# Two small sync-queue loads for 16 partitions of one weight piece in a decode kernel

## The chip, the core and the metric

The kernel runs on one core of a Trainium2 chip. Its time is the device time of one execution in microseconds (us); the figure used is the median over several runs. The core has a matrix engine (PE, with its weight loads PEld), a vector engine (DVE), a scalar engine (ACT), a general engine (POOL) and a sync engine (SP). Transfers between HBM and the on-chip memory SBUF (128 partitions) are issued from SP, ACT or POOL, each with a queue of its own, and are carried out by 16 DMA engines which all queues share. In the profile SP's queue is q1 ("hardware_dynamic"), POOL's is q0 ("software_dynamic"), and q8 and q14 ("instruction") carry the program's own instructions.

## What is computed

The input `x` is 4 rows of 576. It is normalised to `xn`, and the result is the sum of `x`, an attention branch and an MLP branch:

```
xn = layernorm(x)
A: q = xn @ wq ; scores over the last 2048 keys of 16 kv heads ; softmax ; p @ v ; @ wo
B: x1 = xn + hs ; h2 = gelu(layernorm(x1) @ w3) @ w4 ; return x1 + h2
out = x + A + B
```

With one token per sequence the shifted part `hs` of branch B is zero, so `w1` and `w2` are not needed. What the kernel must read is therefore `wq` (4.7 MB), keys and values (67 MB), `wo` (4.7 MB), `w3` and `w4` (5.3 MB each): 87 MB for a few rows of arithmetic.

## The kernel before, in words

Almost all data come in one long stream on POOL's queue. `flush_loads` issues it in the order of the list `order`: keys and values of eight pairs of heads ("K", t and "V", t, each one indirect load of 128 rows of 32 KB, line 125) into three buffers, a quarter of `wo` before every second V (line 147), `w3` after the second V (lines 152 and 153), and last the entry ("W", 0): the last quarter of `wo` and all of `w4`. An entry is issued when a K or V buffer comes free; `free_one`, called twice in each turn of the main loop, says so. SP issues only the two loads of `wq` at the start (lines 142 and 143) and the store of the result at the end (line 716).

`w4` has 4608 rows of 576. Seen as 2 x 128 x 18 rows, each partition holds 36 of them, numbered 0 to 35 in the tile. `load_w4` (line 158) brings them in six pieces, cut at `W4_PIECES` (line 156): rows 0-17, 18-24, 25-29, 30-33, 34 and 35 of every partition. A row is 1152 bytes, so the second piece (number 1) is 7 rows, 8064 contiguous bytes for each of 128 partitions.

The tiles of `wq`, `w3` and `w4` share one buffer (pool `wp`, one buffer, tag "w"), which each takes over from the one before. `w3` is read by `mlp_g` (line 529) in turn `t == G_AT`, that is turn 3 of the main loop; the last of its reads is `mlp_g(2)`. The step `mlp_turn(2)` and the gelu `mlp_act` follow some microseconds later in the same turn. From there on the buffer is empty until `w4` comes.

The end of the kernel is written out by hand (lines 643 to 716). After the last head's values are turned and projected, the matmuls with `w4` follow piece by piece, so that each waits for its own piece only:

```
acc_matmuls(mlp_terms(*W4_PIECES[0:2]))
...
acc_matmuls(mlp_terms(*W4_PIECES[1:3]))
half = sum_open()
sum_matmuls(mlp_terms(*W4_PIECES[2:4]), first=True)
sum_fold(half)
sum_matmuls(mlp_terms(W4_PIECES[3], NF))
```

Then DVE and ACT each copy half of the result (lines 713 and 715) and SP stores it.

Of the kernel before, what the change touches and what calls it, by code (L numbers as in the profile page):

```python
# [11 lines left out]
BF16 = mybir.dt.bfloat16  # L12
# [10 lines left out]
def kernel(  # L23
# [14 lines left out]
    nc = tc.nc  # L38
    P = 128
    B, Sq, D = A_x.shape  # L40
# [4 lines left out]
    F = B_w3.shape[1]  # L45
    assert Sq == 1 and Dh == P and rep == 2 and B == 4 and D == 576
    KJ = 4
    NQ = Hq * Dh
    NF = F // P
    NFH = NF // 2  # L50
# [27 lines left out]
    wp = ctx.enter_context(tc.tile_pool(name="w", bufs=1))  # L78
# [12 lines left out]
    w_tiles = {}  # L91
# [62 lines left out]
        w_tiles["w3"] = t  # L154

    W4_PIECES = [0, NFH, NF - 11, NF - 6, NF - 2, NF - 1, NF]

    def load_w4():
        t = wp.tile([P, NF, D], BF16, tag="w", name="w4_sb")
        src = B_w4.rearrange("(e p i) n -> e p i n", e=2, p=P)  # L160
        for lo, hi in zip(W4_PIECES, W4_PIECES[1:]):
            e, at = divmod(lo, NFH)
            nc.gpsimd.dma_start(out=t[:, lo:hi, :], in_=src[e][:, at:at + hi - lo, :])  # L163
        w_tiles["w4"] = t

    order = [("K", 0), ("K", 1)]
    for t in range(NPR):
# [126 lines left out]
    def k_transpose(t, q):  # L294
        src = kv_tiles["K", t][:].bitcast(I32)[:, q * QC:(q + 1) * QC, :].rearrange("p c (ib i) -> p ib c i", i=QD)
        kt = ktp.tile([P, 2, QC, QD], I32, tag="kt")
        nc.vector.transpose(out=kt[:], in_=src)  # L297
        kts[t, q] = kt
# [3 lines left out]
    for kb in range(NQD):  # L302
        nc.gpsimd.tensor_copy(out=sel[:, :, :, kb, :],
                              in_=ident_bf[:].rearrange("p (ib i e) -> p ib e i", ib=2, e=2))
# [23 lines left out]
    for g in range(2):  # L328
        nc.gpsimd.tensor_copy(out=same_j[:, g * 2 * QD:(g + 1) * 2 * QD].rearrange("p (e s j) -> p e s j", e=2, j=NJ),
                              in_=sel_j[:].unsqueeze(2).to_broadcast([P, 2, NSL, NJ]))  # L330
# [41 lines left out]
    for r in range(2):  # L372
        nc.vector.tensor_copy(out=q_bf[:, r],  # L373
                              in_=qT_ps[:, r].rearrange("p u (g x) -> p g u x", g=NQD)[:, :, :, 0:B])
    qs_ps = ps_m.tile([P, Hkv, 4, rep, B], F32, tag="m", name="qs_ps")
    for ie in range(4):
        ib, e = divmod(ie, 2)
        nc.tensor.matmul(out=qs_ps[:, :, ie], lhsT=sel[:, ib, e].rearrange("p k i -> p (k i)"),
                         rhs=q_bf.rearrange("p r g u b -> p (r g u b)"), start=True, stop=True)
    for kb in range(NQD):  # L380
        rows = slice(kb * QD, (kb + 1) * QD)
        dst = qz[rows, ZP:].rearrange("p (t i m) -> p t i m", i=4, m=P)[:, :, :, kb * QD:kb * QD + NJ]
        src = qs_ps[rows].rearrange("p (t e) i r b -> p e t i (r b)", e=2)[:, kb // 2]
# [13 lines left out]
    def k_mask(t, u):  # L397
        S_ps[t, u] = ps_s.tile([P, NW], F32, tag="S", name="S")
        nc.tensor.matmul(out=S_ps[t, u][:].rearrange("p (c k) -> p c k", k=QD), lhsT=ohT[:],  # L399
                         rhs=negbig[:].unsqueeze(1).to_broadcast([B, SC, QD]),  # L400
                         start=True, stop=False, skip_group_check=True)

    def k_scores(t, q, sl):
        u, s = q // 2, q % 2 * 2 + sl
        kt = kts[t, q][:].bitcast(BF16)
        if sl:
            kts.pop((t, q))
        for ie in range(4):
            ib, e = divmod(ie, 2)
            z0 = (t * 4 + ie) * P + ZP - s * NJ  # L410
            nc.tensor.matmul(out=S_ps[t, u][:], lhsT=qz[:, z0:z0 + P],  # L411
                             rhs=kt[:, ib, sl * SC:(sl + 1) * SC, e:2 * QD:2].rearrange("p c k -> p (c k)"),
                             start=False, stop=False, skip_group_check=True)

    def sm_max(t, u):
        mx = small.tile([P, 1], F32, tag="mx")
        nc.vector.reduce_max(out=mx[:], in_=S_ps[t, u][:], axis=AX.X)  # L417
        if u == 0:
            st["dm", t] = small.tile([P, NU, NG], BF16, tag="dm", name="dm")
        nc.vector.tensor_scalar(out=st["dm", t][:, u, :], in0=sel_g[:], scalar1=mx[:, 0:1], scalar2=None, op0=ALU.mult)  # L420
# [7 lines left out]
    def sm_neg(t):  # L428
        nm = small.tile([2 * NJ, 1], BF16, tag="nm")
        nc.vector.reduce_max(out=nm[:], in_=st.pop(("mg", t))[:], axis=AX.X, negate=True)  # L430
        st["nm", t] = nm
# [46 lines left out]
    def o_scale(t):  # L478
        O_sb[t] = bigp.tile([P, NSL, Dh], F32, tag="big", name="O_sb")
        nc.scalar.activation(out=O_sb[t][:], in_=O_ps.pop(t)[:], func=ACT.Copy, scale=st.pop(("rd", t))[:, 0:1])  # L480
# [48 lines left out]
    def mlp_g(r):  # L529
        w3 = w_tiles["w3"]  # L530
        chunks = G_CHUNKS[r * NQD:(r + 1) * NQD]
        n = chunks[0][2]
        g_ps = (ps_o if r < 2 else ps_m).tile([P, P, n], F32, tag="O" if r < 2 else "m", name="g_ps")
        for j in range(KJ + 1):
            for g, (e, i0, _) in enumerate(chunks):
                base, k = (j * F + e * (F // 2), j) if j < KJ else (KJ * F, KJ + e)
                cols = w3[:, base:base + F // 2].rearrange("p (q i) -> p q i", q=P)
                nc.tensor.matmul(out=g_ps[g * QD:(g + 1) * QD], lhsT=ln2T[:, k, :], rhs=cols[:, :, i0:i0 + n],  # L538
                                 start=(j == 0), stop=False, skip_group_check=True)
        m = len(chunks) * QD  # L540
        g_sb[r] = bigp.tile([P, P, n], F32, tag="g", name="g_sb", bufs=1)
        nc.scalar.activation(out=g_sb[r][0:m], in_=g_ps[0:m], func=ACT.Copy)

    def mlp_turn(r):
        chunks = G_CHUNKS[r * NQD:(r + 1) * NQD]
        n, m = chunks[0][2], len(chunks)
        gT_all = ps_m.tile([P, n * m, QD], F32, tag="m", name="gT_ps")
        gT_ps = gT_all[:].rearrange("p (u g) x -> p u g x", u=n)
        gs = g_sb.pop(r)
        for u in range(n):  # L550
            nc.tensor.transpose(out=gT_ps[:, u].rearrange("p g x -> p (g x)"), in_=gs[0:m * QD, :, u],
                                identity=ident_f[0:m * QD, 0:m * QD])
        if r < 2:
            dst = xs[:, r * NFH:r * NFH + 16, :].rearrange("p (g u) b -> p u g b", u=n)
        else:
            dst = xs[:].rearrange("p (g c) b -> p c g b", c=NFH)[:, 16:18]
        nc.vector.tensor_copy(out=dst, in_=gT_ps[:, :, :, 0:B])

    def mlp_act():
        u = const.tile([P, NF, B], F32, name="g_u")  # L560
        nc.gpsimd.tensor_tensor(out=u[:], in0=xs[:], in1=xs[:], op=ALU.mult)
        nc.gpsimd.tensor_scalar(out=u[:], in0=u[:], scalar1=GELU_A, scalar2=1.0, op0=ALU.mult, op1=ALU.add)
        nc.gpsimd.tensor_tensor(out=u[:], in0=u[:], in1=xs[:], op=ALU.mult)
        nc.scalar.activation(out=u[:], in_=u[:], func=ACT.Tanh, scale=GELU_C)
        nc.gpsimd.tensor_scalar(out=u[:], in0=u[:], scalar1=0.5, scalar2=0.5, op0=ALU.mult, op1=ALU.add)
        nc.gpsimd.tensor_tensor(out=gT[:], in0=u[:], in1=xs[:], op=ALU.mult)
# [8 lines left out]
    for t in range(NPR - 1):  # L575
        a, o = t - 1, t - 2
        if a >= 0:
            sm_max(a, 1)
        if o >= 0:
            o_scale(o)  # L580
        k_transpose(t, 1)
        if t == G_AT:
            mlp_g(0)
        k_mask(t, 0)
        k_scores(t, 0, 0)
        if a >= 0:
            sm_maxT(a)
            sm_neg(a)
        k_scores(t, 0, 1)
        if a >= 0:  # L590
            sm_back(a)
            sm_bias(a)
            sm_exp(a, 0)
            sm_exp(a, 1)
        k_transpose(t, 2)
        if t == G_AT:
            mlp_g(1)
            mlp_turn(0)
        k_scores(t, 1, 0)
        if o >= 0:  # L600
            o_turn(o)
        k_scores(t, 1, 1)
        if a >= 0:
            sm_turn(a, 0)
        if o >= 0:
            o_sum(o)
        k_transpose(t, 3)
        free_one()
        if a >= 0:
            sm_turn(a, 1)  # L610
        if t == G_AT:
            mlp_g(2)
            mlp_turn(1)
        k_mask(t, 1)
        k_scores(t, 2, 0)
        if a >= 0:
            sm_den(a)
            sm_rec(a)
            pv(a, 0, 0, SC // 2)
        k_scores(t, 2, 1)  # L620
        sm_max(t, 0)
        if o >= 0:
            o_spread(2 * o + 1)
        if a >= 0:
            pv(a, 0, SC // 2, SC)
        if o >= 0:
            o_pick(2 * o + 1)
        if t == G_AT:
            mlp_turn(2)
            mlp_act()  # L630
        if t + 1 < NPR:
            k_transpose(t + 1, 0)
        k_scores(t, 3, 0)
        if a >= 0:
            pv(a, 1, 0, SC // 2)
        k_scores(t, 3, 1)
        if a >= 0:
            pv(a, 1, SC // 2, SC)
            free_one()
        if o >= 0:  # L640
            o_proj(2 * o + 1)
# [57 lines left out]
    o_spread(2 * hl + 1)  # L699
    acc_matmuls(mlp_terms(*W4_PIECES[0:2]))  # L700
    o_pick(2 * hl + 1)
    o_proj(2 * hl + 1)
# [6 lines that stand above are left out]
# [38 lines left out]
```

## Time and profile before

| | |
|---|---|
| median of 3 runs | 210.86 us (210.72 to 211.22) |
| the profiled execution, its own time | 211.11 us |
| its span, first to last instruction | 209.3 us |
| granted PE clock, mean | 0.876 |
| PE / DVE / ACT / POOL busy | 144.9 / 124.8 / 29.7 / 31.6 us |
| moved by DMA | 87.32 MB, mean 417 GB/s |
| POOL's queue (q0) | 82.45 MB, 91.8% of 16 engines |
| SP's queue (q1) | 4.72 MB, 5.4% of 16 engines |

The span is what the views below are counted in: 0 is the first instruction of the program. The profiled execution's time is 1.8 us more than its span, for what lies around the instructions. "DMA share" is how busy the 16 DMA engines were on average in a stretch. A DMA issue has a length on the engine that issues it, and lands later: the time to landing counts from the issue, so it includes the wait behind all that the queue already holds.

Beside the grouped views the trace keeps a record of each DMA packet (queue, bytes, start and duration, but not which of the 16 engines carried it) and of each completion: a transfer spread over 16 engines has 16 completions, one per engine, and counts as landed with the last.

### The profile page before, as it was taken

What the parts mean: (1) busy time and instruction counts of PE and PEld (TensorE: products, weight loads), DVE (VectorE), ACT (ScalarE), POOL (GpSimd) and SP (SyncE); (2) the same over time, 40 slices, a digit from 0 to 9 for tenths busy, and PEclk for the clock granted to TensorE, in tenths of its full rate; (3) what the DMA queues carried; (4) which work ended last, traced back from release to release, by engine and by line L of the source; (5) the groups of instructions that cost most, each with busy time, mean ns of one, the idle gap of its engine ahead of it and who ended that gap; (6) DMA issues with size and microseconds to landing.
All of it is one profiled execution on the core that took longest, in us unless ns stands there. A gap on an engine that the chain in (4) does not pass through costs nothing.

```text
span 209.3 us, 2197 instructions
## 1 busy us (share of the span) xinstructions
PE 144.9 (69%) x894; PEld 58.4 (28%) x894; DVE 124.8 (60%) x177; ACT 29.7 (14%) x61; POOL 31.6 (15%) x63
## 2 busy tenths in 40 slices
PE   0249199649679943059996894687957937996954
PEld 0013033222215310014442431143314311443432
DVE  5410779994189700097928990989089818987110
ACT  6402500110102011003001201020002010203100
POOL 5680001003200110000133011001010161100000
PEclk9999859996957995558999999597999996997899
DMA  7999999999999999999999999999999999999991
GB/s 301 401 463 438 401 463 423 438 401 451 451 396 437 447 416 413 392 441 482 413 404 465 432 407 409 477 432 407 457 438 404 446 445 413 438 451 401 419 403 70
DMA packets 4155, 87.32 MB, mean 417 GB/s; under 512 B 488, under 2 KB 496, under 8 KB 1200
## 3 DMA queue, kind: packets, MB, share of 16 engines
q0 software_dynamic: 3840, 82.45, 91.8%
q1 hardware_dynamic: 296, 4.72, 5.4%
q8 instruction: 7, 0.11, 0.2%
q14 instruction: 4, 0.03, 0.0%
q10 hardware_dynamic: 8, 0.00, 0.0%
HBM read 87.17 MB, written 0.00 MB: 416 GB/s over the span
## 4 chain that ended last, share of the span: by engine, by line
DMA 62%; PE 18%; DVE 14%; POOL 2%; issue 2%; ACT 0%; POOLq 0%; DVEq 0%
DMA kn<-in_A_k_cache_dram,row 46%; DMA w_sb<-in_B_w_dram 16%; PE S L411 11%; DVE kt L297 9%; PE O L475 6%; DVE pt L456 1%; POOL w_sb L163 1%; DVE mx L417 1%; PE sum L252 1%; POOL vn L125 0%; PE oT L486 0%; DVE on L496 0%; POOL rstd L268 0%; POOL wo_sb L147 0%; DVE row L116 0%
## 5 line engine op out<-in xcount | busy, mean ns | idle before, releaser
L411 PE MATMUL S<-kt,qz 128*128 128x512 bf16 x256 | 78.4, 439 | 33.4 <-DVE kt L297 33.4
L297 DVE STREAM_TRANSPOSE kt<-kn 128x2048 int32<-128x2048 int32 x32 | 73.7, 2307 | 46.5 <-DMA kn<-in_A_k_cache_dram,row 44.2
L411 PEld LDWEIGHTS <-qz 128*128 128x128 bf16 x256 | 23.4, 104 | 72.6 <-issue 55.8
L475 PE MATMUL O<-vn,pt 128*64 128x512 bf16 x256 | 36.0, 412 | 5.5 <-DVE kt L297 2.5
L456 DVE STREAM_TRANSPOSE pt<-E 64x512 bf16<-64x512 bf16 x32 | 22.1, 690 | 1.2 <-ACT E L447 0.9
L447 ACT ACTIVATE E<-S,bias 128x512 bf16<-128x512 f32 x16 | 10.9, 683 | 75.6 <-DVE bias L440 75.6
L125 POOL DMA_INDIRECT vn<-in_A_v_cache_dram,row x8 | 7.7, 961 | 91.6 <-DVE kt L297 87.5
L475 PEld LDWEIGHTS <-pt 128*64 128x64 bf16 x256 | 13.5, 116 | 22.5 <-issue 13.8
L480 ACT ACTIVATE O_sb<-O,rd 128x512 f32<-128x512 f32 x8 | 5.5, 687 | 62.5 <-PE O L475 62.5
L125 POOL DMA_INDIRECT kn<-in_A_k_cache_dram,row x8 | 7.9, 989 | 42.4 <-PE O L475 23.2
L417 DVE TENSOR_REDUCE mx<-S 128x1 f32<-128x512 f32 x16 | 10.7, 668 | 0.1
L538 PE MATMUL g_ps<-w_sb,ln2T 128*32 128x512 bf16 (+1 forms) x50 | 5.2, 486 | 2.9 <-DMA w_sb<-in_B_w_dram 2.9
L399 PE MATMUL S<-negbig,ohT 4*128 4x512 bf16 x16 | 6.4, 398 | 0.0
L486 PE MATMUL oT<-ident_w,O_sb 128*128 128x128 f32 x32 | 5.2, 286 | 0.0
L355 PE MATMUL q_ps<-wq_sb,xnT 128*32 128x512 bf16 x40 | 4.5, 631 | 0.9 <-DMA wq_sb<-in_A_wq_dram 0.9
L496 DVE TENSOR_REDUCE on<-oT 128x16 bf16<-128x128 f32 x8 | 2.3, 287 | 4.4 <-PE oT L486 4.2
L486 PEld LDWEIGHTS oT<-ident_w,O_sb 128*128 128x128 f32 x32 | 4.1, 149 | 2.2 <-issue 0.9
L163 POOL DMA_DIRECT2D w_sb<-in_B_w_dram x6 | 3.3, 585 | 8.2 <-DMA vn<-in_A_v_cache_dram,row 8.2
L440 DVE TENSOR_SCALAR bias<-bp 128x1 f32<-128x1 f32 x8 | 1.3, 158 | 5.2 <-PE bp L435 5.2
L713 DVE CAST fin<-sum 4x288 bf16<-4x288 f32 x1 | 0.4, 446 | 6.5 <-PE sum L252 6.5
L420 DVE TENSOR_SCALAR dm<-sel_g,mx 128x8 bf16<-128x8 bf16 x16 | 3.9, 243 | 0.6
L373 DVE COPY first<-qT_ps 128x64 bf16<-128x64 bf16 x2 | 0.3, 186 | 6.6 <-PE qT_ps L370 6.6
(103 smaller groups left out, 83.1 us busy)
## 6 DMA issues: line engine op xcount, KB each, us to landing
wo_sb<-in_A_wo_dram POOLq DMA_DIRECT2D x4, 1152.0 KB, 23.6
w_sb<-in_B_w_dram POOLq DMA_DIRECT2D x1, 4608.0 KB, 29.5
wq_sb<-in_A_wq_dram SPq DMA_DIRECT2D x1, 4096.0 KB, 13.8
w_sb<-in_B_w_dram POOLq DMA_DIRECT2D x1, 2592.0 KB, 29.1
w_sb<-in_B_w_dram POOLq DMA_DIRECT2D x2, 576.0 KB, 31.7
w_sb<-in_B_w_dram POOLq DMA_DIRECT2D x1, 1008.0 KB, 31.0
w_sb<-in_B_w_dram POOLq DMA_DIRECT2D x1, 720.0 KB, 32.2
wq_sb<-in_A_wq_dram SPq DMA_DIRECT2D x1, 512.0 KB, 3.3
```

The lines of the kernel that those rows point to most:

```text
L125: nc.gpsimd.indirect_dma_start(tl[:].rearrange("p c d -> p (c d)"), None, k_rows if kind == "K" else v_rows, bass.IndirectOffsetOnAxis(ap= ...
L163: nc.gpsimd.dma_start(out=t[:, lo:hi, :], in_=src[e][:, at:at + hi - lo, :])
L297: nc.vector.transpose(out=kt[:], in_=src)
L399: nc.tensor.matmul(out=S_ps[t, u][:].rearrange("p (c k) -> p c k", k=QD), lhsT=ohT[:], rhs=negbig[:].unsqueeze(1).to_broadcast([B, SC, QD] ...
L411: nc.tensor.matmul(out=S_ps[t, u][:], lhsT=qz[:, z0:z0 + P], rhs=kt[:, ib, sl * SC:(sl + 1) * SC, e:2 * QD:2].rearrange("p c k -> p (c k)" ...
L417: nc.vector.reduce_max(out=mx[:], in_=S_ps[t, u][:], axis=AX.X)
L447: nc.scalar.activation(out=E[t, u][:].rearrange("p c k -> p (c k)"), in_=S_ps.pop((t, u))[:], func=ACT.Exp, scale=scale, bias=st["bias", t ...
L456: nc.vector.transpose(out=pts[t % 2 * NU + u][rows, :, e * QD:(e + 1) * QD], in_=e_in[rows])
L475: nc.tensor.matmul(out=O_ps[t][rows], lhsT=pts[t % 2 * NU + u][:, c, :], rhs=vn[:, u, :, c, :], start=(u == 0 and c < 2), stop=False, skip ...
L480: nc.scalar.activation(out=O_sb[t][:], in_=O_ps.pop(t)[:], func=ACT.Copy, scale=st.pop(("rd", t))[:, 0:1])
L486: nc.tensor.transpose(out=oT[:, s, :], in_=o[:, s, :], identity=ident_w[:, s * NJ:s * NJ + P])
L538: nc.tensor.matmul(out=g_ps[g * QD:(g + 1) * QD], lhsT=ln2T[:, k, :], rhs=cols[:, :, i0:i0 + n], start=(j == 0), stop=False, skip_group_ch ...
```

## The change

The piece number 1 of `w4` (rows 18 to 24) is loaded in three parts. Partitions 0 to 111 still come in the stream on POOL's queue, at the same place in the order. Partitions 112 to 119 and 120 to 127 come by two loads of 8 partitions each, issued by SP; in the program they stand in turn 3 of the main loop, between `mlp_turn(2)` and `mlp_act()`. The tile of `w4` is therefore taken there, and no longer in `load_w4`; it has the same number of elements as before (4 x 4608 + 2304 = 36 x 576). The other five pieces and all matmuls are as they were.

```
     W4_PIECES = [0, NFH, NF - 11, NF - 6, NF - 2, NF - 1, NF]
+    W4_LOW = 1
+    LOW = 8
+    w4_src = B_w4.rearrange("(e p i) n -> e p i n", e=2, p=P)
+
+    def w4_load(queue, piece, rows):
+        lo, hi = W4_PIECES[piece:piece + 2]
+        e, at = divmod(lo, NFH)
+        queue.dma_start(out=w_tiles["w4"][rows, lo:hi, :], in_=w4_src[e][rows, at:at + hi - lo, :])
+
+    def load_w4_low():
+        w_tiles["w4"] = wp.tile([P, KJ * F + F // 2], BF16, tag="w", name="w4_sb")[:].rearrange("p (i n) -> p i n", n=D)
+        for p0 in range(P - 2 * LOW, P, LOW):
+            w4_load(nc.sync, W4_LOW, slice(p0, p0 + LOW))
 
     def load_w4():
-        t = wp.tile([P, NF, D], BF16, tag="w", name="w4_sb")
-        src = B_w4.rearrange("(e p i) n -> e p i n", e=2, p=P)
-        for lo, hi in zip(W4_PIECES, W4_PIECES[1:]):
-            e, at = divmod(lo, NFH)
-            nc.gpsimd.dma_start(out=t[:, lo:hi, :], in_=src[e][:, at:at + hi - lo, :])
-        w_tiles["w4"] = t
+        for piece in range(len(W4_PIECES) - 1):
+            w4_load(nc.gpsimd, piece, slice(0, P - 2 * LOW if piece == W4_LOW else P))
...
             mlp_turn(2)
+            load_w4_low()
             mlp_act()
```

## The prediction

> **What bounds the kernel now.** I read first the page's fourth part, the chain that ended last. It gives 62% of the span to DMA.
>
> ```profile
> DMA packets 4155, 87.32 MB, mean 417 GB/s; under 512 B 488, under 2 KB 496, under 8 KB 1200
> ...
> q0 software_dynamic: 3840, 82.45, 91.8%
> q1 hardware_dynamic: 296, 4.72, 5.4%
> q8 instruction: 7, 0.11, 0.2%
> q14 instruction: 4, 0.03, 0.0%
> ...
> DMA 62%; PE 18%; DVE 14%; POOL 2%; issue 2%; ACT 0%; POOLq 0%; DVEq 0%
> ```
>
> The reader should see that one queue, POOL's, fills the 16 DMA engines for 91.8% of the span, and that the program's own instructions take 7 and 4 packets of their own. Next the same chain in order of time, from 164.8 us on:
>
> ```profile
> 169.35 0.94 POOL vn L125
> 170.29 0.00 issue
> 170.29 0.58 POOL wo_sb L147
> 170.87 1.56 POOL w_sb L163 x3
> 172.43 33.10 DMA w_sb<-in_B_w_dram
> 205.54 0.04 issue
> 205.58 1.06 PE sum L252 x12
> 206.63 0.43 DVE fin L713
> ```
>
> From 172.43 us to 205.54 us the chain is the landing of `w4`; after its last byte only 1.06 us of matmuls, the 0.43 us copy and the store remain. So the last of 16 completions, at 205.54, sets the end. Third, the busy time by stretches, near the end (columns: stretch, length, five engines' busy time, PE clock, DMA share, GB/s):
>
> ```profile
> 200.00:205.00 5.00, 3.23 (x78) 2.14 (x79) 0.17 (x1) 0.41 (x1) 0.00 (x0) 1.00 0.94 389
> ...
> 204.00:205.00 1.00, 0.81 (x12) 0.54 (x13) 0.00 (x0) 0.00 (x0) 0.00 (x0) 1.00 0.73 284
> 205.00:206.00 1.00, 0.87 (x12) 0.40 (x10) 0.00 (x0) 0.00 (x0) 0.00 (x0) 1.00 0.32 129
> ```
>
> DMA share falls to 0.73 and then 0.32 before the last byte: the engines don't finish together. The completion records of the last row give it exactly: six engines end at 203.82 to 204.12, two at 204.32 and 204.70, eight at 205.21 to 205.54. Their mean is 204.78.
>
> What made eight engines late shows in the packet records. The first late engine appears right after the 16384-byte instruction packet at 31.98 us (0.93 us, and the next stream packet of that engine 0.83 us instead of 0.35), and each of the 7 packets of q8 and some of q14 adds to one engine. An engine once late by 1.3 to 1.4 us is still late at the end, because the queue is never empty (DMA share 0.99, 1.01 and 0.98 over the first 100, the next 70 and the next 35 us). So time lost by an engine anywhere in mid-stream is there at the end.
>
> **The change, part by part.** *Removed:* one partition in eight of piece 1. Its 128 packets of 8064 bytes took 0.305 us each, 8 on each engine. With 112 rows over 16 engines (my estimate, 112/16 = 7) each engine saves one: -0.305 us.
>
> *Added:* two loads of 8 rows. The four-row loads of this trace (x at the start, the result at the end) gave one packet and one completion to each of four engines. By that row an 8-row load gives one packet of 8064 bytes to each of eight engines; whether both loads use the same eight is not seen, and I take it so. Each of these eight carries two foreign packets in mid-stream and is spared one. Price of one: from below 0.305 us, the stream's own packet of that size; the change from `wq`'s queue to the first keys near 13 us shows no longer packets (1.21 to 1.22 us for 32 KB before and after), so a change of queue can be free. From above the four 8192-byte instruction packets, lone packets of another queue between stream packets: 0.488, 0.309, 0.309 and 0.309 us, and the engine's next 32 KB packet took 1.578, 1.427, 1.579 and 1.744 instead of 1.213. That is 0.85, 0.52, 0.68 and 0.84 us, mean 0.72. This is the nearest row in size, place and kind, so I take 0.72. For eight engines: 2 x 0.72 - 0.305 = **+1.14 us** (ends: +0.305 and 2 x 0.85 - 0.305 = +1.40). For the other eight: -0.305 us.
>
> Which of these reaches the end depends on which engines are late. Eight of sixteen are. The end is moved by +1.14 as soon as one of the latest is among the eight that take the new loads; it falls by 0.305 only if the eight are just the other, early ones, whose 204.70 and 204.12 would then be 205.84 and 205.26 at my price, or 205.01 at the lower. I see no engine numbers in the trace; by chance alone such a clean split is rare.
>
> [...] In this trace the four x rows, which go to four neighbouring partitions at once, took 48 to 56 ns for 1152 bytes each, no more than alone by the stream's rate (1152 / 8064 x 305 = 44 ns, and 9 ns for a mere completion packet), so no crowding is seen, on a very small load. [...]
>
> *Moved: SP.* SP does nothing but wait for the result from the start on.
>
> ```profile
> SPq L716 <- DVE fin L713: 205.5, 1, 205.5
> ```
>
> So the two issues (0.35 us, by the store's issue) delay nobody; the store, behind them on SP, is due 100 us later. They must wait until the buffer's `w3` has been read:
>
> ```profile
> 99.72 1.31 PE L538 MATMUL g_ps<-w_sb,ln2T 128*32 128x256 bf16 x10
> ```
>
> These matmuls end at 101.0, so the loads go out there and run at about 101 to 104 us, amid a stream with DMA share 0.97 (100 to 105 us): there is no idle DMA time to hide in. If SP were later, up to 170 us, the price would be the same.
>
> *POOL.* It issues six `w4` loads as before, and its one wait among them (8.2 us for an earlier value load) stays; that wait ends 24 us before the landing it concerns. A wait for SP's loads, if one is added, was met 65 us earlier: nothing.
>
> *PE.* The 14 matmuls of piece 1 now need three landings. They start at 202.44 us, after 0.66 us of waiting for POOL's part, so the early parts cost nothing; without that cover a met semaphore costs a few hundredths of a microsecond. They end at 203.1, and what follows waits for the later pieces in any case.
>
> Sum: +1.14 us. The profiled execution took 211.11, its span 209.3 plus 1.8 around it, 0.25 above the median; the same shift on the median 210.86 gives **212.0 us**. About 0.2% (0.42 us) is what a measurement of this kernel can tell from no change.
>
> **Rivals.** *(a) The 112-row load runs badly.* The stream's 128-row loads always finish a row in step on all engines; for 112 rows the rows must be dealt out anew, and nothing in the trace shows such a load. [...]
>
> *(b) It evens the engines out, and is not slower.* If all late engines are among the eight that are only spared, the latest end 0.305 earlier: 210.56. It decides at a price per foreign packet below about 0.42 us, because 204.70 + 2p - 0.305 must stay under 205.24; at a mean price of 0.72 the early six (204.12) would reach 205.26 and only the 204.70 engine would pass it, to 205.84. No dealing of the same bytes can gain more than 205.54 - 204.78 = 0.76 us, 210.1. For it: exactly eight engines are late. Against: the instruction packets hit engines one after another, and nothing says they keep to one half.
>
> *(c) Nothing to measure.* The price is at the lower end and late engines lie in both halves: +0.305, 211.2.
>
> **How the numbers follow.** Forecast (+0.5 to +1.4): 0.45. Rival (a), +1.5 to +3.3: 0.18. Rival (b), -0.76 to -0.2: 0.22, of which about 0.12 beyond 0.42 us (that needs more than the worked 0.305, so I count part of it only). Rival (c), within 0.42: 0.15. Slower by over 0.2%: 0.43 of the forecast and all of (a), 0.61; same 0.27; faster 0.12. The range leaves out the best of (b) and the worst of (a): 210.4 to 213.5. The forecast's own range is 211.3 to 212.3.
>
> **What would show it.** In the part on DMA issues, piece 1 at 882 KB (112 x 8064 bytes) and two issues of 63 KB on SPq, landing within a few microseconds of 101; q1 with 32 more packets. The packets after the two loads show whether the next 32 KB packet takes 1.2 or 1.4 to 1.7 us: that is the price. In the last row's completions, the spread of 1.72 us grows to about 2.9 if late engines were loaded, and shrinks below 1.5 under (b). Packets of 8064 bytes near 200 us longer than 0.305 would show (a). The prediction is wrong if foreign packets on SP's queue are cheap, or if the eight engines are just the early ones.

## The result: 217.21 us, and the profile after

The changed kernel took 217.21 us (median of 6 runs, 216.32 to 217.79) beside 210.85 us for the kernel before (6 runs, 210.72 to 211.22): a ratio of 1.0295, 95% interval 1.0278 to 1.0313, so +6.36 us (5.9 to 6.6). The forecast was 212.0 with a range of 210.4 to 213.5: the right sign, and far too little.

The profiled execution took 216.77 us, its span 215.0 plus 1.8 around it; that is 5.66 us more than the profiled execution before. The page's lines on the DMA queues and on the chain that ended last:

```profile
DMA packets 4171, 87.32 MB, mean 406 GB/s; under 512 B 504, under 2 KB 512, under 8 KB 1216
...
q0 software_dynamic: 3824, 82.32, 91.5%
q1 hardware_dynamic: 328, 4.85, 5.5%
q8 instruction: 7, 0.11, 0.2%
q14 instruction: 4, 0.03, 0.0%
...
DMA 63%; PE 23%; DVE 9%; POOL 2%; issue 1%; ACT 0%; POOLq 0%; DVEq 0%
```

The same 87.32 MB move; only the mean rate falls, from 417 to 406 GB/s. q1 has gained 32 packets: 16 of data and 16 completions. The same chain in order of time, its end:

```profile
172.13 0.00 issue
172.14 0.58 POOL wo_sb L147
172.72 1.63 POOL w_sb L164 x3
174.34 36.85 DMA w_sb<-in_B_w_dram
211.20 0.04 issue
211.24 1.07 PE sum L261 x12
212.31 0.43 DVE fin L723
```

The chain is built as before: a landing of `w4`, then 1.07 us of matmuls and the 0.43 us copy. The landing that the chain names is that of rows 30 to 33; rows 34 and 35, for which the last of these twelve matmuls wait, land 0.36 and 0.72 us behind it (205.90 and 206.26 before, 211.58 and 211.93 now), and the copy starts 0.36 us after the last one in both kernels. But the landing in the chain ends at 211.20 and not at 205.54, and those 5.66 us are the whole difference of the two profiled executions. So the question is only why the transfers took longer. What SP waited for, and what the new loads and the shortened one moved, from the page's part on DMA issues:

```profile
SPq L726 <- DVE fin L723: 111.2, 1, 111.2
SPq L164 <- DMA w_sb<-in_B_w_dram: 77.1, 1, 77.1
SPq L164 <- PE g_ps L547: 21.9, 1, 21.9
```

```profile
w_sb<-in_B_w_dram POOLq DMA_DIRECT2D x1, 882.0 KB, 35.1
```

SP waited for `w3`'s landing and its readers, then issued both loads at 100.82 us, and then waited for the result: nothing was behind them. They landed at 108.00 and 111.72 us. The stream's part is 882 KB, 112 rows. The work by stretches (stretch, length, five engines' busy time, PE clock, DMA share, GB/s), first the kernel before and then the changed one, around the two SP loads and around the 112-row load:

```profile
103.00:110.00 7.00, 7.00 (x53) 2.99 (x53) 2.74 (x9) 0.32 (x1) 2.38 (x6) 1.00 0.93 400
197.00:204.00 7.00, 4.29 (x98) 2.81 (x96) 1.43 (x4) 0.90 (x2) 0.00 (x0) 1.00 0.99 414
```

```profile
103.00:110.00 7.00, 7.00 (x52) 2.90 (x50) 2.49 (x9) 0.32 (x1) 2.13 (x6) 1.00 1.00 316
197.00:204.00 7.00, 4.20 (x46) 2.22 (x43) 1.43 (x4) 0.69 (x1) 0.00 (x0) 0.93 0.99 309
```

Read the last two columns together. The DMA share is 1.00 and 0.99, so the engines hardly idle; the rate drops from 400 to 316 and from 414 to 309 GB/s. The packets became longer. The packet records say which (their times are counted from the span's start, as in the views):

- At 104.39 to 105.16 and again at 108.00 to 108.75 eight packets of 8064 bytes of q1 appear, most of them at 0.305 us, the stream's own price. But the 32 KB packet of all 16 engines beside the first load took 2.0 to 2.2 us (one 1.76) instead of 1.21, and beside the second 2.15 to 2.5 (two 1.65 and 2.01). All time of the stream's packets above their usual duration, summed from 103 to 111 us and divided by 16, is 1.80 us per engine.
- The 112 stream packets of 8064 bytes took 0.541 us on average (0.305 to 0.907) instead of 0.305; the pieces beside them suffer too: 5760 bytes 0.348 instead of 0.220, 20,736 bytes up to 1.90 instead of 0.771. It lasts on all engines from the first one that enters the 112-row load (about 199.5) to the last that leaves it (about 207.3). From 195 to 211 us that is 3.30 us per engine.

The last row's completions went from 204.53 to 206.26 (mean 205.50) to 209.04 to 211.93 (mean 210.25). The mean moved nearly as far as the last one: all engines lost, not eight. (The prediction has the completions of the kernel before 0.72 us earlier, because it counted packets and completions from a zero 0.72 us later than that of the views.)

### The profile page after: what moved, and what is told of

It is laid out like the page before. It is cut to its first block, busy times and chain, and to the rows that moved or that the text cites. A ratio compares the mean times of both kernels' runs of the same rounds, so it can differ in the third digit from the quotient of the medians.

```text
span 215.0 us, 2203 instructions
## 1 busy us (share of the span) xinstructions
PE 148.5 (69%) x894; PEld 59.1 (27%) x894; DVE 124.7 (58%) x177; ACT 29.7 (14%) x61; POOL 31.6 (15%) x63
## 2 busy tenths in 40 slices
DMA packets 4171, 87.32 MB, mean 406 GB/s; under 512 B 504, under 2 KB 512, under 8 KB 1216
## 4 chain that ended last, share of the span: by engine, by line
DMA 63%; PE 23%; DVE 9%; POOL 2%; issue 1%; ACT 0%; POOLq 0%; DVEq 0%
DMA kn<-in_A_k_cache_dram,row 46%; DMA w_sb<-in_B_w_dram 17%; PE S L420 15%; DVE kt L306 6%; PE O L484 6%; POOL w_sb L164 1%; PE oT L495 1%; PE sum L261 0%; PE S L408 0%; POOL vn L125 0%; DVE mx L426 0%; POOL rstd L277 0%; POOL wo_sb L147 0%; DVE row L116 0%; POOL dup L288 0%
## 5 line engine op out<-in xcount | busy, mean ns | idle before, releaser
L420 PE MATMUL S<-kt,qz 128*128 128x512 bf16 x256 | 81.7, 454 | 36.3 <-DVE kt L306 36.3
L420 PEld LDWEIGHTS <-qz 128*128 128x128 bf16 x256 | 23.9, 106 | 74.9 <-issue 59.3
L484 PE MATMUL O<-vn,pt 128*64 128x512 bf16 x256 | 35.3, 407 | 4.2 <-DVE kt L306 2.4
L239 PE MATMUL acc<-w_sb,gT 128*4 128x288 bf16 x50 | 2.8, 374 | 3.7 <-DMA w_sb<-in_B_w_dram 3.7
```

The source lines that it names most:

```text
L420: nc.tensor.matmul(out=S_ps[t, u][:], lhsT=qz[:, z0:z0 + P], rhs=kt[:, ib, sl * SC:(sl + 1) * SC, e:2 * QD:2].rearrange("p c k -> p (c k)" ...
L484: nc.tensor.matmul(out=O_ps[t][rows], lhsT=pts[t % 2 * NU + u][:, c, :], rhs=vn[:, u, :, c, :], start=(u == 0 and c < 2), stop=False, skip ...
```

## The experiments

The trace does not say which engine carried a packet or which partitions it wrote, so the runs change those two things one at a time. The theories, by the letters of the expectations: A, both parts of the change cost and add up; W, several engines that write the same few groups of neighbouring partitions at one time slow the stream; Q, a packet of another queue costs by the change of queue; R, it is the source rows in HBM, which lie close together; and that a row count other than 128 is bad in itself. From the run with the upper half on, W also supposes that each engine has partitions of its own to write (the expectations' "usual engine" and "own group"); that is the author's supposition, and no trace here shows which engine writes what. Differences are between medians, each to the kernel before run beside it (210.81 to 211.09). The profile lines are windows as above; a window's rate also depends a little on when the next keys were issued, so small differences are read from the packet records.

### One part of the change at a time

The SP loads alone: they stay, and the stream's load is whole again, so that 16 partitions are written twice.

```
-            w4_load(nc.gpsimd, piece, slice(0, P - 2 * LOW if piece == W4_LOW else P))
+            w4_load(nc.gpsimd, piece, slice(0, P))
```

> The two 8-row loads of the sync queue stay, but the stream's own load of piece 1 covers all 128 partitions again, so 16 partitions come twice. In the changed kernel's packet records the 32 KB packet that each of the 16 engines carried next to the first of these loads took 2.03 to 2.2 us instead of 1.21, and 2.15 to 2.5 next to the second. Theory A (both parts cost, each for itself): 0.8 + 1.0 + 0.3 for the bytes on eight engines, so +1.9 to +2.3 us on before, 212.8 to 213.2. Rival B (the loss comes from the 112-row load alone, and engines held up at 104 us make it good later): +0.0 to +0.4, 210.9 to 211.3. Both: packets of 8064 bytes on the stream's queue are back at 0.305 us.

Measured: 213.22 us, +2.41, ratio 1.0114 (1.0097 to 1.0131). All stream packets of 8064 bytes are back at 0.305 us; 63 packets of 32 KB are long between 103 and 111 us, 1.73 us per engine. The stretch of the loads and the chain's end:

```profile
103.00:110.00 7.00, 6.93 (x52) 3.01 (x53) 2.83 (x9) 0.32 (x1) 2.47 (x6) 1.00 1.06 363
```

```profile
174.05 33.56 DMA w_sb<-in_B_w_dram
207.61 0.04 issue
207.66 1.06 PE sum L261 x12
208.72 0.44 DVE fin L723
```

The last row's completion is 2.08 us late (208.34) although it is 100 us after the loads: what an engine loses in mid-stream is still lost at the end, as the prediction had it. Each packet starts within a few ns of the end of the one before on its engine (3 to 4 ns for most between 99 and 112 us in the changed kernel), so packets can be followed along an engine: the 16 packets of the two loads fall on the same eight engines, two on each.

The 112-row load alone: no SP loads; the tile is taken in `load_w4` again, and the product of piece 1 runs over 112 partitions, so that the kernel leaves 16 partitions of these seven rows out of its result.

```
-        for p0 in range(P - 2 * LOW, P, LOW):
-            w4_load(nc.sync, W4_LOW, slice(p0, p0 + LOW))
...
+        n = P - 2 * LOW if (lo, hi) == tuple(W4_PIECES[W4_LOW:W4_LOW + 2]) else P
+        return [(gT[0:n, u, :], w4[0:n, u, :]) for u in range(lo, hi)]
```

> No sync-queue loads; the stream's load of piece 1 covers 112 partitions, and the product of its 7 rows uses these 112 partitions only, so 16 of 128 partitions of 7 rows are left out of the result. Theory A: the changed kernel's 6.36 us less the 2.1 of the sync loads, +3.8 to +4.4 on before, 214.7 to 215.2, with stream packets of 8064 bytes at about 0.54 us and its neighbours slowed as well. Rival B: nearly all of it, +5.9 to +6.4. Rival C (112 rows are dealt 7 to an engine and run at the usual rate): -0.3, 210.5.

Measured: 214.45 us, +3.64, ratio 1.0158 (1.0137 to 1.018), with fewer bytes moved than before. The stretches at the end:

```profile
197.00:204.00 7.00, 4.43 (x86) 2.87 (x85) 1.43 (x4) 0.69 (x1) 0.00 (x0) 0.92 0.97 246
...
204.00:208.00 4.00, 2.27 (x24) 1.12 (x25) 0.00 (x0) 0.41 (x1) 0.00 (x0) 0.50 0.81 305
```

246 GB/s at a DMA share of 0.97; packets of 8064 bytes at 0.523 us. The last completion is at 209.20, +2.93. The remaining 0.7 us come behind it: PE, at a granted clock of 0.50 from 204 to 208 us, has fallen behind the landings, and the copy starts 1.11 us after the last completion instead of 0.36.

Theory A holds: 2.41 + 3.64 = 6.05 of 6.36, inside that difference's interval. By the last completion it is 2.08 + 2.93 = 5.01 of 5.67; the 0.66 between is left open.

### What makes the SP loads dear

All of these keep the stream's load whole, as in the first run, and change only what SP's loads write or read (the stream's load writes the same partitions again later). Other target partitions, four apart, same source rows:

```
+            nc.sync.dma_start(out=w_tiles["w4"][32 * k:32 * k + 32:4, lo:hi, :],
+                              in_=w4_src[1][p0:p0 + LOW, lo - NFH:hi - NFH, :])
```

> As the run with sync loads and a full stream load, but each 8-row sync load writes to partitions 4 apart (0, 4, ... 28 and 32, 36, ... 60) instead of 8 neighbours; the rows that it reads are the same, and the stream's load writes these partitions again later. Theory W (many engines writing into few neighbouring groups of partitions slow all engines): the slow 32 KB packets at 104 and 107 us are gone, and +0.3 to +0.6 on before is left, 211.2 to 211.5. Rival Q (a lone packet of another queue stalls the engines, wherever it writes) and rival R (reading 8 rows that lie close together in HBM does it): as with neighbours, +1.9 to +2.3.

Measured: 211.45 us, +0.64, ratio 1.0029 (1.0019 to 1.0039). No 32 KB packet beside the loads is longer than 1.213 us, the next packet of a carrying engine neither (one of 1.68 follows an instruction packet, as in the kernel before):

```profile
103.00:110.00 7.00, 6.93 (x52) 3.01 (x53) 2.78 (x9) 0.32 (x1) 2.42 (x6) 1.00 0.98 419
```

419 GB/s against 363. A lone packet of SP's queue cost just its own 0.305 us here; two per carrying engine are 0.61, and the medians show 0.64 (the profiled execution's last completion is only 0.24 later, but it is set against a profiled execution of the kernel before that took 0.26 us more than its median). Q is out. Followed from packet to packet, the two last completions (206.33, 206.50) belong to engines that carried the loads.

Other source rows, 16 apart, targets as in the change:

```
+            nc.sync.dma_start(out=w_tiles["w4"][p0:p0 + LOW, lo:hi, :],
+                              in_=w4_src[1][k // LOW * 4:P:16, lo - NFH:hi - NFH, :])
```

> As the run with sync loads and a full stream load, with the same 8 neighbouring partitions written, but the rows read lie 16 partitions' rows apart in w4 (0, 16, ... 112 and 4, 20, ... 116). Theory W and rival Q: as with near rows, +1.9 to +2.3 us on before. Rival R (near rows in HBM): +0.3 to +0.6, and the 32 KB packets beside the loads are back at 1.21 us.

Measured: 213.31 us, +2.50, ratio 1.0118 (1.0101 to 1.0135); 64 long packets, 1.74 us per engine, the same as with neighbouring source rows. R is out for these loads: it is the written side.

```profile
103.00:110.00 7.00, 6.93 (x52) 3.00 (x53) 2.78 (x9) 0.32 (x1) 2.43 (x6) 1.00 0.99 333
```

Three more arrangements of the same 16 packets. One load of 16 rows to partitions 112 to 127 (`w4_load(nc.sync, W4_LOW, slice(P - 2 * LOW, P))`):

> As the run with two 8-row sync loads and a full stream load, but the 16 rows come by one sync load to partitions 112 to 127: one packet on each of 16 engines, four packets into each of four groups of four partitions. The two 8-row loads cost 2.41 us, 1.2 each, which is 4 x 0.305 us, four packets of one group one after the other; the loads to spread partitions cost 0.64, which is 2 x 0.305. Theory W with that price (packets per group x 0.305, paid by all engines): +1.2 us on before, 212.0, half of the two loads, though the bytes are the same. Rival V (the price goes by the crowded bytes): +2.4, 213.2. Rival E (one packet more on each engine and nothing else): +0.3, 211.1.

Measured: 212.40 us, +1.44, ratio 1.0070 (1.0053 to 1.0087); 0.77 us per engine. Four packets per group at 0.305 us are 1.2.

```profile
103.00:110.00 7.00, 7.00 (x58) 2.83 (x58) 2.00 (x6) 0.39 (x2) 2.04 (x5) 1.00 1.01 377
```

Two loads of 8, each to every second of the partitions 112 to 127 (`out=w_tiles["w4"][P - 2 * LOW + k:P:2, lo:hi, :]`), so two packets per group of four partitions and load:

> Two 8-row sync loads to partitions 112, 114, ... 126 and 113, 115, ... 127 and a full stream load: two packets into each of four groups of four partitions, where the changed kernel's loads put four into each of two. Theory W with the price of packets per group x 0.305: 2 x 2 x 0.305 = +1.2 us on before, 212.0, halfway between 213.2 (four per group) and 211.45 (one). Rival (any two engines on one group slow all alike): as with four, +2.4.

Measured: 212.76 us, +1.80, ratio 1.0112 (1.0071 to 1.0154); 32 KB packets of 1.57 to 1.82 us, 0.97 us per engine. By the packets this is less than with four per group (0.97 against 1.73 us per engine); the times alone don't separate the two, as one of the four runs took 214.44 us and the intervals overlap. It is more than the 1.2 that packets per group times 0.305 us gives.

```profile
103.00:110.00 7.00, 7.00 (x53) 3.00 (x53) 2.73 (x9) 0.32 (x1) 2.39 (x6) 1.00 1.05 391
```

Targets four apart again, but in the upper half (64 to 92, then 96 to 124; `64 + 32 * k:96 + 32 * k:4`):

> Two 8-row sync loads to partitions 64, 68, ... 92 and 96, 100, ... 124 and a full stream load: one packet per group of four, like the loads to partitions 0 to 60, but into the groups of the upper 64 partitions. If the eight engines that carry the loads usually write the lower 64 partitions, each packet now meets the group's usual engine. Theory W: the carriers and the usual engines share a group for 0.61 us per load: +0.6 to +1.2 on before, 211.4 to 212.0, and 32 KB packets of about 1.5 us beside the loads on all or half of the engines. Rival (only how many packets a load puts into a group counts, not whose group it is): as with the lower partitions, +0.64, 211.45, and 32 KB packets at 1.21.

Measured: 212.21 us, +1.25, ratio 1.0062 (1.0045 to 1.0079); 40 packets of 32 KB are long, most of them 1.37 to 1.64 us, 0.59 us per engine.

```profile
103.00:110.00 7.00, 7.00 (x62) 2.91 (x62) 1.91 (x6) 0.49 (x2) 2.04 (x5) 1.00 1.00 391
```

One packet per group here as in the lower half, and yet twice the price (+1.25 beside +0.64): it matters not only how many packets a group gets but also which half of the partitions they go to. Why, no trace shows.

### What makes the stream's load dear

The kernel before with piece 1 in two loads of 64 partitions, lower and upper half, both on POOL's queue, no SP load at all:

```
+            for rows in [slice(0, P // 2), slice(P // 2, P)] if lo == NFH else [slice(0, P)]:
+                nc.gpsimd.dma_start(out=t[rows, lo:hi, :], in_=src[e][rows, at:at + hi - lo, :])
```

> No sync loads; the stream brings piece 1 by two loads of 64 partitions (0 to 63 and 64 to 127) in place of one of 128. [...] Theory W for the stream's own loads: packets of 8064 bytes at about 0.61 us on all engines, 2 x 4 x 0.61 - 2.44 = +2.4 us, and up to +4 with the neighbouring pieces slowed meanwhile: 213.2 to 214.8. Rival (it is the row count 112, 7 packets to an engine, that is bad, and 64 rows run as usual): 0 to +0.1, 210.9, packets at 0.305.

Measured: 216.38 us, +5.42, ratio 1.0251 (1.0227 to 1.0275), for the same bytes on the same queue. The last completion is 4.87 us late, and here too PE comes behind it: from rows 25 to 29 on, PE is what the chain runs through, and the copy starts 1.21 us after the last completion. Packets of 8064 bytes take 0.594 us on average, nearly 2 x 0.305:

```profile
197.00:204.00 7.00, 3.22 (x54) 2.16 (x56) 1.43 (x4) 0.69 (x1) 0.00 (x0) 0.91 1.00 233
```

```profile
172.36 36.63 DMA w_sb<-in_B_w_dram
209.00 0.04 issue
209.04 0.87 PE sum L253 x10
209.91 0.96 PE sum L258 x4
210.87 1.48 PE sum L253 x12
```

So 112 is not a special number. The 0.61 us of the expectation was the author's estimate, twice the 0.305 of the trace; 0.594 was measured. By theory W, what 64 neighbouring partitions and 112 have in common is that several engines work on the same share of the partitions; no trace shows it. To tell this from "fewer rows are bad", the same two loads as combs, even partitions and odd partitions:

```
-            for rows in [slice(0, P // 2), slice(P // 2, P)] if lo == NFH else [slice(0, P)]:
+            for rows in [slice(0, P, 2), slice(1, P, 2)] if lo == NFH else [slice(0, P)]:
```

> Piece 1 of w4 comes by two loads of 64 partitions on POOL's queue, as in the run with the two halves, but the first takes the even partitions and the second the odd ones. [...] Rival H (a load of fewer than 128 rows, or two loads in place of one, runs badly whatever its partitions): 0.5 to 0.6 us per packet and +4 to +5.5 us, as with the two halves (+5.42).

Measured: 210.92 us beside 211.09, ratio 0.9992 (0.9983 to 1.0001): no difference, where the halves cost 5.42. Every packet of 8064 bytes is at 0.305 us.

```profile
w_sb<-in_B_w_dram POOLq DMA_DIRECT2D x2, 504.0 KB, 29.4
```

```profile
197.00:204.00 7.00, 4.93 (x102) 3.14 (x99) 1.43 (x4) 1.10 (x2) 0.00 (x0) 1.00 0.95 397
```

Two loads, 64 rows each, the same sizes: only the partitions differ, and with them the rows that each load reads, and the rate is 397 instead of 233 GB/s. W, which had packets of 0.305 us and at most +0.4 us here, holds against the rival. (That the rows read do not matter was shown for SP's loads only; for the stream's loads no run separates the two.) Not every comb is free, as the next two show.

The change itself in combs of every eighth partition: SP brings 7, 15, ... 127, POOL's queue seven loads of 16.

```
+        w4_load(nc.sync, W4_LOW, slice(LOW - 1, P, LOW))
...
+            for rows in [slice(k, P, LOW) for k in range(LOW - 1)] if piece == W4_LOW else [slice(0, P)]:
+                w4_load(nc.gpsimd, piece, rows)
```

> The change with the same bytes on the same two queues, dealt otherwise: SP brings one load of 16 partitions, every eighth one (7, 15, ... 127), and POOL's queue the other 112 as seven loads of 16 partitions (0, 8, ... then 1, 9, ... up to 6, 14, ...). Theory W: each engine has one row of each load, in its own group, eight packets of 8064 bytes per engine as before, 0.305 us each, and no slow neighbours at 101 to 111 us: time of the kernel before to +0.5 us (six more issues and completions). If fewer rows on POOL's queue or rows on SP's queue cost in themselves: +1.4 (the SP load of 16 neighbouring partitions alone) to +6.4 us (the change).

Measured: 214.68 us, +3.59, ratio 1.0195 (1.0166 to 1.0223). This missed the 0.5 us, for two reasons that the run does not separate. The small packets took 0.45 us on average, up to 0.63; and the many loads held up POOL (the waits from 170 us on):

```profile
202.00:204.00 2.00, 1.66 (x36) 1.14 (x39) 0.00 (x0) 0.00 (x0) 1.42 (x3) 0.67 0.58 152
```

```profile
POOL w_sb L164 <- DMA vn<-in_A_v_cache_dram,row: 17.8, 2, 9.6
POOL w_sb L164 <- DMA w_sb<-in_B_w_dram: 7.2, 1, 7.2
POOL w_sb L164 <- DMA wo_sb<-in_A_wo_dram: 2.2, 1, 2.2
```

POOL's loads signal their landing on eight semaphores in turn (106 to 113 in the records of the kernel before and of the changed one), and each load waits until the one eight places before it has landed: in the kernel before, the last load of `w4`, on 109, goes out at 181.74 us, after the value load on 109 has landed at 181.46. With six loads more, POOL waited four times where it had waited once, and last 7.2 us for the first piece of `w4`, before it issued the rest at 202.58 us. At 202 to 204 us the DMA share is 0.58: for once the engines ran dry.

The SP load of that comb alone, beside the whole stream load:

```
-        w4_load(nc.sync, W4_LOW, slice(P - 2 * LOW, P))
+        w4_load(nc.sync, W4_LOW, slice(LOW - 1, P, LOW))
```

> As the run with one SP load of the 16 partitions 112 to 127 beside the full 128-row load (+1.44 us), but the SP load takes every eighth partition (7, 15, ... 127): the same 16 packets of 8064 bytes in mid-stream, one per engine. Theory W: each engine stays in its own group, so only the extra packet remains, +0.3 us (0.2 to 0.6), and the 32 KB packets beside it stay at 1.21 us. Rival (a packet of SP's queue slows the stream whatever it writes): +1.4 us again.

Measured: 212.00 us, +0.91, ratio 1.0037 (1.0025 to 1.005). Better than 16 neighbours (+1.44), but not the +0.3 of the expectation: 32 KB packets of 1.29 to 1.63 us.

```profile
103.00:110.00 7.00, 7.00 (x52) 2.92 (x54) 2.57 (x9) 0.32 (x1) 2.22 (x6) 1.00 0.98 391
```

Why a packet costs more in this comb than in the lower half four apart (+0.91 for 16 packets in one load, +0.64 for 16 in two) is not shown: no trace here has engine numbers or the partitions of a packet. The last run brings piece 1 by both queues again, in combs of every second and every fourth of the 128 partitions. That these keep the engines apart was the author's supposition; what the run can show is the time and the packets.

```
+        w4_load(nc.sync, W4_LOW, slice(0, P, 4))
...
+            for rows in [slice(1, P, 2), slice(2, P, 4)] if piece == W4_LOW else [slice(0, P)]:
+                w4_load(nc.gpsimd, piece, rows)
```

> [...] SP brings one load of 32 partitions (0, 4, ... 124) in mid-stream, POOL's queue the odd partitions (64) and then 2, 6, ... 126 (32). Corrected theory W: two packets per engine beside the keys, six in the stream, each 0.305 us, the 32 KB packets at 101 to 111 us stay at 1.21 us, time of the kernel before to +0.5 us. [...] If a mid-stream load on SP's queue costs in itself, whatever it writes: +1.2 us or more with packets of 0.305 us in the stream's part.

Measured: 211.10 us beside 210.86, ratio 1.0008 (0.9999 to 1.0017): within what can be told from no change. SP carries 32 packets here, twice as many as in the change, all at 0.305 us; the 32 KB packets beside them are at 1.21 (but the one behind an instruction packet), the stream's 96 packets of 8064 bytes at 0.305.

```profile
q1 hardware_dynamic: 344, 4.98, 5.7%
```

```profile
103.00:110.00 7.00, 6.94 (x52) 2.96 (x53) 2.71 (x9) 0.32 (x1) 2.35 (x6) 1.00 0.98 418
197.00:204.00 7.00, 4.43 (x98) 2.95 (x98) 1.43 (x4) 1.04 (x2) 0.00 (x0) 1.00 0.96 402
```

418 and 402 GB/s where the change has 316 and 309. All of the loss came from which partitions the pieces were cut at, and none from the second queue, the mid-stream place or a load of fewer than 128 rows as such (112 rows in another arrangement were not run). It does not gain either: the same bytes still pass the 16 engines.

### The runs side by side

| what differs from the kernel before | time, us | last completion, later by |
|---|---|---|
| the change | +6.36 | 5.67 |
| SP loads alone, 8 + 8 neighbours | +2.41 | 2.08 |
| the same, other source rows | +2.50 | 2.07 |
| the same, two per group and load | +1.80 | 1.41 |
| SP load of 16 neighbours | +1.44 | 1.17 |
| SP loads four apart, upper half | +1.25 | 0.83 |
| SP load, every eighth partition | +0.91 | 0.87 |
| SP loads four apart, lower half | +0.64 | 0.24 |
| 112-row load alone | +3.64 | 2.93 |
| two halves | +5.42 | 4.87 |
| two combs | -0.17 | -0.01 |
| seven combs, and SP's | +3.59 | 2.99 |
| SP's comb of 32, and two combs | +0.24 | -0.05 |

The times are medians; the last column compares single profiled executions, and the one of the kernel before took 0.26 us more than its median.

## Why the prediction was right or wrong

**What bounds the kernel: right in the main.** The landing of `w4`'s last rows set the end in the changed kernel and in most runs. In the 112-row load alone and in the two halves PE added 0.75 and 0.85 us behind it, and in the seven combs POOL's late issue stood in the chain. One reading was off: the prediction took 205.54 us in the chain for the landing of the last row, but that is rows 30 to 33, and the last row lands at 206.26. Its list of completions for the last row also ends at 205.54 only because of its other zero. So 0.36 us, and not 1.06, lie between the last completion and the copy; the shift that it forecast is not touched by this.

**SP, POOL and PE at no cost: right.** The loads went out at 100.82 us and SP had nothing behind them (they landed 7 to 11 us later, not within a few). POOL's last issues came with the stream, 1.9 us later than before, and were no longer (0.58 and 1.63 us beside 0.58 and 1.56). On PE a wait that had long been met took 51 ns (for SP's second load, at 205.79 us), among the matmuls before piece 1. The rest after the landing in the chain is 1.07 and 0.43 us as before.

**Time lost in mid-stream stays lost: right** (2.08 us at the last completion, 100 us after the SP loads).

**The removed packet, -0.305 us: the term that failed most.** Each engine does carry seven packets instead of eight, but they cost 0.541 us each: 7 x 0.541 = 3.79 instead of 8 x 0.305 = 2.44, so +1.35 where the sum had -0.305; and the pieces beside them, whose packets the sum left as they were, lose as much again (3.30 us per engine in all, 7 x 0.236 = 1.65 of it on these packets). The whole term measured +2.93 at the last completion and +3.64 in time when run alone.

**Rival (a) came true, and was priced and weighted too low.** It had +1.5 to +3.3 with the loads, at 0.18. No run shows the term behind these numbers; the runs showed 0.541 us instead of 0.305 for the packets of the 112-row load (0.523 with that load alone), and the neighbouring pieces slowed as well (5760 bytes 0.348 instead of 0.220). A load whose kind "nothing in the trace shows" was a reason for a wide range, not for a small chance: the stream's loads in the trace were all of 128 rows, so the cost of another dealing was not bounded by any row.

**The foreign packet, 0.72 us on eight engines: size and mechanism wrong.** A lone packet between stream packets cost 0.305 us, the lower end (+0.64 for two). The instruction packets, the row taken as nearest, delay their engine by more (0.52 to 0.85 us), and no run here tests why; the price is not that of changing queues. What the SP loads cost comes with eight neighbouring partitions per load (+2.41, and +0.64 four apart in the lower half): 1.73 to 1.80 us on all 16 engines, where the step had 1.44 on eight (the same eight for both loads, as it assumed) and nothing on the other eight. In the sum it came to +1.14 with the spared packet; alone it measured +2.41.

**The x rows against crowding: too weak a row.** The prediction saw no crowding in the x load's 48 to 56 ns. Those rows of 1152 bytes came at 1.67 to 1.72 us, before the first 32 KB packet of the stream at 13.09 us, and could not show what 8064 bytes to each of eight neighbouring partitions cost in a full stream: +2.41 for two such loads.

**Rival (b), an even finish and no loss: rightly left out of the sum, and late engines were among the eight.** With four-apart targets the two last engines were carriers. It took no part in the result.

**What would show it.** The sign for (a), stream packets of 8064 bytes longer than 0.305, came true. The spread of the last row's completions grew to 2.90 us as forecast, but that agreement is empty: the mean moved by 4.75 us, where the step gives 2 x 0.72 / 2 - 0.305 = +0.42. The mean of the completions, not their spread, tells whether some or all engines lose.

## What to carry to other kernels

Before a load in a full DMA stream is cut by partitions, ask which partitions each part will write, and run it: here blocks of neighbouring partitions cost +2.41 us (8 and 8 beside the stream), +3.64 (112) and +5.42 (64 and 64), combs of every second partition nothing (-0.17), and combs of every second and every fourth over both queues nothing that can be told (+0.24); but the combs of every eighth cost +0.91 and +3.59. Pieces cut along the free dimension, 128 partitions each, ran at 0.305 us per 8064 bytes in the kernel before. A DMA share near 1 with a falling rate meant here that packets had become longer (1.00 at 316 GB/s, with 32 KB packets of 2.0 to 2.5 us instead of 1.21): look at packets of the same size before and after. Where the trace has only one kind of load, a load of another shape is unbounded by it, and the range has to say so.

## What the runs showed of the hardware

- A load to 8 partitions of 64.5 KB lengthened the current 32 KB packet of all 16 engines from 1.21 us to 2.0 to 2.5 us in nearly all cases, though its eight packets fell on eight of them. Why the other eight are slowed is not shown.
- 64 neighbouring partitions in place of 128: 0.594 us per packet and +5.42 us for 1 MB; 64 partitions as a comb: 0.305 us and nothing. Both are two loads to disjoint halves of the partitions: what they cost depends on which halves.
- Two queues in one stream cost nothing beyond their bytes in the last run (+0.24 us, within what can be told from no change): 32 packets of SP's queue between the 32 KB packets of keys and values, all at 0.305 us, those at 1.21.
- Seven loads of 126 KB in place of one made POOL wait 7.2 us for an earlier landing, and the DMA share fell to 0.58. The wait is the program's doing (eight semaphores in turn, 106 to 113) and not the engines'.
